# Seven half products for half of gate and value, f32 first loads by SyncE, and fixed orders, in an attention and gated feed-forward kernel

## Chip, core and metric

The kernel runs on one core of one Trainium2 chip. The metric is the device time of one execution in microseconds (us). An execution is profiled apart from the timed ones; its span runs from its first to its last instruction.

## What is computed

Attention over 4 batches, 8 heads, 768 positions and 64 dimensions; three heads (0, 2, 6) are causal over all keys, the other five see only the first 4 keys and a window of 64. Its output, as 3072 tokens of 512, goes through a gated feed-forward layer with a gated residual:

```python
scores = scale * np.matmul(q, k.transpose(0, 1, 3, 2))      # masked, softmax -> a
x = np.matmul(a, v)                                         # -> (3072, 512)
g = x @ w_gate                                              # (512, 1536)
gelu = 0.5 * g * (1.0 + erf(g * inv_sqrt2))
val = x @ w_val                                             # (512, 1536)
ffn_out = gelu * val @ w_out                                # (1536, 512)
res_gate = 1.0 / (1.0 + np.exp(-(x @ w_res)))               # (512, 512)
return x + res_gate * ffn_out
```

## The kernel before

The 3072 tokens are cut into six chunks of 512 (`CHUNKS`, L25; counted from 0 here). For each chunk the kernel computes scores (`scores`, L858), exponentials on ScalarE (L909), masks on VectorE (L945), weighted values on TensorE and normalisation (`weigh`, L998; L1082, L1084), a transposition of x to features (`to_features`, L1104, on TensorE, or by DMA at L1097), gate and value (`gate_value`, L1121), sums of the hidden tile (`sums`, L1175), and output (`output_fast`, L1212; `output`, L1295, for the first two tiles of chunk 0). The text calls TensorE, VectorE, ScalarE, GpSimd and SyncE by the profile's PE, DVE, ACT, POOL and SP as well.

**Gate and value.** Twelve blocks f of 128 features, and for each block four matmuls (one per 128 of the 512 inputs) of 512 tokens for gate and four for value, each in a PSUM bank. ScalarE takes GELU of the gate (L1166), VectorE multiplies it with the value into hT (L1168). In chunk 0 the first four blocks go in two halves of 256 tokens (L1140, L1143).

**Output.** `output_fast` already uses seven half products in place of eight (Strassen's scheme in the form of Winograd) for two tiles of 128 tokens at a time: sums S1 to S4 of hT (L1187), sums T1 to T4 of w_out made once (L1204), products of 256 columns into two PSUM banks, and, between them, copies out of PSUM (`keep`, L1251 and L1252) and additions (`plus`, L1257). Then comes the gate of the residual from tanh (L1226, L1281), the addition of x (L1286) and a store by SyncE (L1292).

**Tiled matmuls.** `mm` (L513) issues a matmul whole (L516) or, when the planner has put the task in column mode, as two of 64 columns of weights each that run beside each other (L517).

**Loads.** Chunks 0 and 1 load queries and keys through GpSimd's DMA queue (L577 is the helper's line for all its DMAs), cast to f16 on the way, and transpose them on TensorE (L709, evicted at L723); later chunks load by GpSimd and transpose by SyncE's DMA (L754). Values and weights come through GpSimd's queue too. While TensorE has nothing else to do at the start, it runs matmuls on a blank tile (L1333).

**Order.** Every instruction or small group is a task with a cost, a priority, buffers and dependencies. `schedule` (L219) replays the kernel in time with the costs of the functions at L458 to L471 and, whenever an engine is free, takes the ready task of the lowest priority; for tasks that several engines can do (`flex`) it picks the one that ends it first. `HINTS` (L46) overrides some priorities. The result is one fixed order for each engine; `assign_waits` and `emit` turn dependencies into semaphore waits. Each engine runs its order without overtaking.

Of the kernel before, what the change touches and what calls it, by code (L numbers as in the profile page):

```python
# [43 lines left out]


HINTS = (  # L46
    "3:-58.9 11:-130.04 428:854.14 430:718.61 444:2782.08 457:-821.9 460:407.45 490:4205.68 521:1522.06 "
    "591:-818.43 610:-36.63 612:486.89 613:-2965.25 619:1544.03 621:-44.07 643:467.87 644:-881 646:4.3 656:119.6 "
    "664:25.04 673:629.62 675:-109.25 695:-2674.26 696:-1856.67 703:-881.5 706:-108.75 707:714.39 708:1939.7 "
    "711:270.02 712:497.18 716:476.22 720:652.56 738:638.32 743:520.23 744:3053.24 749:514.3 750:1799.28 "  # L50
    "751:2383.53 756:521.28 762:1469.72 764:4344.87 767:2237.74 787:-603.93 815:5053.25 817:2978.67 821:1231.87 "
    "824:1484.86 836:2402.62 837:798.1 841:706.04 848:-288.52 849:2997.07 876:2751.74 906:2555.54 913:1516.93 "
    "918:2437.99 919:1519.88 924:1537.25 931:1510.23 936:2384.32 949:2443.79 955:2089.28 967:2846.74 995:-227.38 "
    "1001:29.83 1002:3171.86 1003:3180.29 1004:1146.58 1007:2686.58 1012:1781.89 1040:-803.29 1043:1907.45 "
    "1045:1028.83 1046:667.33 1050:3229.28 1051:1536.45 1053:3573.03 1056:-1823.77 1084:4090.27 1110:2454.97 "
    "1111:2597.62 1117:2808.38 1123:2507.5 1128:2481.58 1129:2529.63 1134:2508.5 1146:2434.73 1152:2779.33 "
    "1153:3034.61 1158:3861.94 1165:2795.06 1171:3076.63 1176:2997.8 1185:5989.69 1188:2243.92 1189:2528.84 "
    "1192:2789.39 1193:2537.45 1194:3836.22 1208:3021.15 1215:6294.68 1263:3219.13 1268:5037.38 1283:4420.5 "
    "1308:4756.92 1311:3513.6 1317:3517.03 1321:3052.3 1329:5930.49 1330:3507.5 1335:3508.5 1336:3519.22 "
    "1341:4624.14 1345:3444.6 1353:3516.64 1354:3538.83 1357:2761.66 1365:3787.63 1366:5173.04 1372:5102.72 "  # L60
    "1386:5438.32 1392:4014.31 1393:4933.66 1418:5146.68 1430:4133.91 1441:5428.8 1452:5127.54 1457:2188.42 "
    "1462:4595.33 1464:5711.23 1467:9389.54 1468:4425.54 ~1471:550.69 1476:5611.77 1499:4504.13 1513:6742.83 "
    "1516:5340.27 1522:4510.5 1523:4585.63 1526:3632.38 1534:4503.02 1539:4253.34 1550:4463.64 1565:7711.51 "
    "1570:4506.5 1571:5085.34 1580:2427.42 1594:2466.44 1610:9272.71 1625:3048.93 1627:6036.71 1629:6167.81 "
    "1631:5064.12 1644:6476.5 1662:4125.72 1671:5044.95 1672:7314.6 1676:4967.2 1683:6427.71 1692:9540.12 "
    "1711:7387.16 1757:5137.62 1784:5507.1 1797:5469.41 1803:7562.23 1817:7773.49 1818:7478.69 1823:7672.83 "
    "1834:7419.08 1836:10250.4 1849:7490.55 "
)

# [121 lines left out]
VS_DMA = 0  # L191
LAT = {"pe": 0.20, "act": 0.10, "dve": 0.08, "pool": 0.12, "sp": 0.1}


class Graph:
# [22 lines left out]

    def schedule(self):  # L219
# [21 lines left out]
        running = []  # L241
        while left:
# [3 lines left out]
            for e in ENGS:  # L246
# [3 lines left out]
                for t in cand[e]:  # L250
# [6 lines left out]
                    key = (int(away), p_, t.seq)  # L257
                    if t.ready > now or (best is not None and key >= bkey):
                        continue
                    if t.alts and any(max(free[f], now) + t.alts[f][0] + BIAS[f] < now + t.alts[e][0] + BIAS[e] - 1e-6  # L260
                                      for f in t.alts if f != e):
                        continue
# [22 lines left out]
                progressed = True  # L285
                if t.name == "g0" and warming:
                    warming = False
                    cand["pe"] = [w for w in cand["pe"] if w.name != "warm"]
                    gone = [w for w in self.tasks if w.name == "warm" and w.end is None]
                    left -= len(gone)  # L290
                    self.tasks = [w for w in self.tasks if w not in gone]
# [109 lines left out]
    def emit(self):  # L401
# [31 lines left out]
        with nc.Block() as blk:  # L433
# [17 lines left out]
            @blk.sync  # L451
            def _(e):
                run("sp", e)
                for t in finals:
                    e.wait_ge(t.sem, 16)
# [6 lines left out]
def c_act(n):  # L462
    return 0.19 + n * 0.000834


def c_dve(n, rate=1.0, psum=True):
    return (0.125 if psum else 0.065) + n * 0.00104 / rate
# [6 lines left out]
def build_kernel(nc, q, k, v, w_gate, w_val, w_out, w_res, out):  # L474
# [11 lines left out]
    scratch = sb("scratch", [128, 1], FP16)  # L486
    blank = sb("blank", [128, 128], FP16)
# [4 lines left out]
    P_vs = Pool(many("vs", 2, [128, NT - 1, NHEAD, DHEAD + 1], FP16))  # L492
    P_vk = Pool(many("vk", 2, [128, 8, DHEAD + 1], FP16))
    P_qkt = Pool(many("qkt", 2, [128, 2, NPAIR, SEQ], FP16))
# [9 lines left out]
    P_hs = Pool(many("hS", 1, [128, 3, NF // 2, 2, 128], FP16))  # L504
    wt = sb("wt", [128, 4, NF // 2, 256], FP16)
    P_ga = Pool(many("gact", 4, [128, 512], FP16))
    P_sr = Pool(many("srs", 3, [128, 512], FP32))
# [5 lines left out]
    def mm(e, o, lhsT, rhs, **k):  # L513
# [8 lines left out]
        "gv": (4, one(6, 7, 5, 4, 3, 2)), "gv0": (4, one(6, 7, 5, 4)), "gvh": (4, one(7, 6, 4, 5)), "out": (2, one(6, 7)), "fin": (4, one(6, 7, 1, 0)), "warm": (1, one(7, 5)),  # L522
# [55 lines left out]

    wtok = {}

    def load_weights():
# [6 lines left out]
        for j in range(4):  # L588
# [3 lines left out]
            wtok["o", j].late = 2.2  # L592
        for nm in "gv":
            for j in range(3):
                wtok[nm, j].late = 2.2 if j else 2.0
# [6 lines left out]
    copies = []  # L602

    def batch(b):
        if b not in batches:
            B_ = B()
            B_.v, B_.vs, B_.vk, B_.qkt = Buf(P_v), Buf(P_vs), Buf(P_vk), Buf(P_qkt)
            B_.vtok, B_.vstok, B_.qtok, B_.ktok = {}, {}, {}, {}

            B_.q6, B_.q6tok = None, {}  # L610
            batches[b] = B_
        return batches[b]

    def values(b, a, z, base, each, on_engines=False):

        BB = batch(b)
        for i in range(a, z):
            BB.vtok[i] = dma("pool", base, 0.9, (lambda i=i: lambda: at(BB.v)[:, i, :, 0:DHEAD])(),
                             v[b, :, i * 128:(i + 1) * 128, :].rearrange("h p d -> p h d"), bufs=[BB.v])
            BB.vtok[i].late = 1.6 if base < 50 else 6.0  # L620
        if a == 0:
# [9 lines left out]
            for t in BB.vktok:  # L631
                t.slack = 12.0 if b else 0.0
# [5 lines left out]
        if on_engines:  # L638
            ts = []
            for lo, hi, pr in ((1, 2, -75),) + (() if VS_DMA else ((2, 4, 130),)):  # L640
                for dst, src, off in ((0, 64, 1), (64, 0, 0)):
                    def vs(on, dst=dst, src=src, off=off, lo=lo, hi=hi):
                        def fn(e):
                            o = at(BB.vs)[dst:dst + 64, lo - 1:hi - 1, :, :].rearrange("p i h d -> p (i h d)")
                            i_ = at(BB.v)[src:src + 64, lo - off:hi - off, :, :].rearrange("p i h d -> p (i h d)")
                            return e.activation(out=o, in_=i_, func=AF.Copy) if on == "act" else e.tensor_copy(out=o, in_=i_)
                        return fn
                    n_ = (hi - lo) * 520
# [9 lines left out]
        for lo in cuts:  # L658
            hi = lo + 1 if each else z
            ts = []  # L660
            for dst, src, off in ((0, 64, 1), (64, 0, 0)):
                ts.append(G.add("sp", 1.2, (lambda lo=lo, hi=hi, dst=dst, src=src, off=off: lambda e: e.dma_start(
                    at(BB.vs)[dst:dst + 64, lo - 1:hi - 1, :, :].rearrange("p i h d -> p (i h d)"),
                    at(BB.v)[src:src + 64, lo - off:hi - off, :, :].rearrange("p i h d -> p (i h d)")))(),
# [7 lines left out]
    def loads_rows(c, si, b, a, z):  # L672
# [17 lines left out]
        for gi, (h0, h1) in enumerate(groups):  # L690
            for j, src in enumerate((q, k)):
                t = dma("pool", base + 4 * gi + j, (h1 - h0) * n * (0.092 if c else 0.089),
# [7 lines left out]
        per = 1 if c == 0 or n == 4 else 2  # L700
        for k_ in range(0, NPAIR, per):
            ps_ = ORDER[k_:k_ + per]
            pr = 1000 * c - 492 + ps_[0] if c else 40 * k_ - 205
            for js in (((1,), (0,)) if c == 0 else ((0, 1),)):
                scr = Buf(P_ps, "scr" if c else "scr0")
                items = [(p, jj) for jj in js for p in ps_]
# [10 lines left out]
                def ev(on, p0=ps_[0], scr=scr, j0=js[0], m=len(items)):  # L717
                    def fn(e):
                        o = at(BB.qkt)[:, :, :, lo:hi].rearrange("c j (y x) w -> c x (j y) w", x=2)[:, p0 % 2]
                        m0 = j0 * 2 + p0 // 2  # L720
                        o = o[:, m0:m0 + m, :].rearrange("c m (p j) -> c m p j", j=n)
# [5 lines left out]
                           bufs=[scr, BB.qkt], name="qkE")  # L727
# [4 lines left out]
    def loads_natural(c, si, b, a, z):  # L732
# [8 lines left out]
        for i in range(a, z):  # L741
            for j, src in ((1, k), (0, q)):
# [9 lines left out]
                for d in ds:  # L752
                    d.late = 5.0
                t = G.add("sp", 1.65, (lambda sv=sv, i=i, j=j: lambda e: e.dma_start(  # L754
                    at(BB.qkt)[:, j, :, i * 128:(i + 1) * 128], sv(), transpose=True))(), ds, base, bufs=[st, BB.qkt], dma=0.85, name="dT")
# [4 lines left out]
            if i == a:  # L760
                values(b, a, z, base, False)
        t = G.add("sp", 0.8, lambda e: e.dma_start(at(BB.q6)[0:64, :, a * 128:z * 128], at(BB.qkt)[64:128, :, 1, a * 128:z * 128]),
                  loaded, base + 1, bufs=[BB.qkt, BB.q6], dma=0.4, name="q6")
        t.late = 1.0
        copies.append(t)
        for i in range(a, z):
            BB.q6tok[0, i] = BB.q6tok[1, i] = t
# [90 lines left out]
    def scores(P, tiles, banks, g, retr):  # L858
# [7 lines left out]
        for bi, (x, blocks, low) in enumerate(banks):  # L866
# [3 lines left out]
            for (b, kt, q0, nq) in blocks:  # L870
# [5 lines left out]
                if kt is None:  # L876
                    deps += [BB.ktok[p, q0]] + ([BB.ktok[p, q0 - 1]] if q0 else [])
                    parts = [(max(0, q0 * 128 - 64 + 64 * s), q0 * 128 + 64 * s, 64, o + 64 * s) for s in range(2)]
                else:
                    deps.append(BB.ktok[p, kt])  # L880
                    parts = [(kt * 128, q0 * 128, nq * 128, o)]
                for i in range(nq):
                    P.where[x, kt, b, q0 + i] = w_ + i * 128
                for (k0, qq, w, oo) in parts:
                    mms.append((lanes[lane], len(mms), BB, half, k0, qq, w, oo, low))
# [5 lines left out]
        def sc(e):  # L891
            side = lambda BB, low, j: at(BB.q6)[:, j, :] if low else at(BB.qkt)[:, j, p, :]
            return [e.matmul(at(scr)[:, oo:oo + w], lhsT=side(BB, low, 1)[half, k0:k0 + 128],  # L893
                             rhs=side(BB, low, 0)[half, qq:qq + w], start=True, stop=True)
                    for (_, _, BB, half, k0, qq, w, oo, low) in mms]
        qkts = [batch(b).qkt for b in dict.fromkeys(b for b, _ in tiles)]
# [548 lines left out]
```

The softmax here doesn't subtract the row's maximum and nothing guards it: scores larger than these inputs give would overflow.

## Time and profile before

| | |
|---|---|
| median of three runs | 265.71 us (265.57 to 266.54) |
| span of the profiled execution | 263.7 us |
| PE, DVE, ACT, POOL busy | 257.7, 181.6, 147.2, 89.3 us |
| bytes read from HBM, written | 29.36 MB, 6.29 MB |
| first matmuls on loaded data | 5.68 us |
| first gate matmuls | 19.72 us |

The profiled execution's time outside its span isn't recorded by itself; the median of the runs lies 2.0 us above the span. Busy time counts overlapping instructions once per engine. A group's line has the code line, engine and operation, the tile written and the tiles read, the shape and the count, then total busy us and mean ns of one, then the engine's idle time just before and who ended it. A matmul's duration includes the time until its last result is out, so matmuls overlap, and the rate is read from the distance of their starts.

### The profile page before, as it was taken

To read this page: it belongs to the slowest core of one execution; us is meant where nothing else is said; L and a number is where in the kernel's file an instruction comes from. 1 tells how busy PE (TensorE), PEld (TensorE's weight loads), DVE (VectorE), ACT (ScalarE), POOL (GpSimd) and SP (SyncE) were. 2 spreads that over 40 slices of the span, in tenths; PEclk is the share of its full clock that TensorE was granted. 3 is DMA by queue.
4 is the path that set the end of the run, shared out by engine and by line. 5 is a ranking of instruction groups with operands and counts; after the bars stand their busy time and mean duration, and the time that the engine had idled before them with its cause. 6 is when DMAs were issued, how large, how long until landed. Compare 5 with 4: busy or idle time off the path is not lost.

```text
span 263.7 us, 7495 instructions
## 1 busy us (share of the span) xinstructions
PE 257.7 (98%) x3226; PEld 164.0 (62%) x3226; DVE 181.6 (69%) x378; ACT 147.2 (56%) x237; POOL 89.3 (34%) x127
## 2 busy tenths in 40 slices
PE   7999999999999999999999999999999999999993
PEld 6777655468444668544567444589655588655692
DVE  2698437798447888557898366888557689837655
ACT  2785467974244987423787242967243888233430
POOL 8999979506109973975000000000000000000003
PEclk9999999999999999999999999999999999999999
DMA  6999999999999999999996110004200004200003
GB/s 83 174 204 206 188 175 231 175 153 204 134 200 148 165 137 177 171 179 176 174 156 150 42 40 0 2 26 101 82 2 0 2 2 122 82 2 0 2 35 127
DMA packets 96513, 29.22 MB, mean 111 GB/s; under 512 B 84449, under 2 KB 93025, under 8 KB 96481
## 3 DMA queue, kind: packets, MB, share of 16 engines
q0 software_dynamic: 70320, 14.69, 67.5%
q1 hardware_dynamic: 26160, 14.07, 28.0%
q8 instruction: 25, 0.41, 0.7%
q14 instruction: 8, 0.06, 0.1%
HBM read 29.36 MB, written 6.29 MB: 135 GB/s over the span
## 4 chain that ended last, share of the span: by engine, by line
PE 95%; DMA 2%; DVE 1%; issue 0%; POOLq 0%
PE ps L516 50%; PE ps L517 32%; PE ps L893 5%; PE ps L1333 2%; PE ps L1017 2%; PE ps L709 2%; DMA qks<-in_q_dram 2%; PE ps L1106 2%; PE ps L984 1%; DVE otile L1281 1%; DVE otile L1286 1%; DVE otile L1257 0%; POOLq L1427 0%
## 5 line engine op out<-in xcount | busy, mean ns | idle before, releaser
L1166 ACT ACTIVATE gact<-ps 128x512 f16<-128x512 f32 x68 | 40.2, 597 | 73.5 <-PE ps L516 43.7
L1168 DVE SCALAR_TENSOR_TENSOR hT<-gact,ps 128x512 f16<-128x512 f16 x68 | 46.1, 686 | 48.0 <-PE ps L516 23.1
L516 PE MATMUL ps<-xT,wg 128*128 128x512 f16 (+1 forms) x208 | 50.0, 363 | 0.0
L516 PE MATMUL ps<-xT,wv 128*128 128x512 f16 (+1 forms) x202 | 49.0, 362 | 0.0
L1286 POOL TENSOR_TENSOR otile<-otile,xtok 128x256 f32<-128x256 f32 x3 | 2.4, 801 | 136.2 <-DVE otile L1281 136.2
L577 POOL DMA_DIRECT2D qks<-in_k_dram x36 | 28.0, 810 | 17.3 <-DMA qkt<-qks 13.9
L516 PEld LDWEIGHTS ps<-xT,wg 128*128 128x128 f16 x208 | 20.1, 98 | 20.0 <-DVE otile L1257 0.3
L516 PEld LDWEIGHTS ps<-xT,wv 128*128 128x128 f16 x202 | 19.4, 98 | 20.0 <-DVE hT L1168 0.5
L577 POOL DMA_DIRECT2D qks<-in_q_dram x36 | 28.4, 828 | 2.2 <-issue 1.4
L517 PE MATMUL ps<-xT,wv 128*64 128x512 f16 x204 | 28.3, 380 | 0.0
L577 POOL DMA_DIRECT2D va<-in_v_dram x24 | 21.3, 920 | 15.1 <-PE ps L516 15.1
L517 PE MATMUL ps<-xT,wg 128*64 128x512 f16 x192 | 26.3, 379 | 0.0
L909 ACT ACTIVATE ea<-ps 128x1024 f16<-128x1024 f32 (+2 forms) x24 | 21.1, 915 | 1.7 <-PE ps L893 1.6
L1257 DVE TENSOR_TENSOR otile<-otile,ps 128x256 f32<-128x256 f32 x33 | 13.6, 417 | 7.1 <-PE ps L517 4.7
L1226 ACT ACTIVATE srs<-ps 128x512 f32<-128x512 f32 x22 | 13.1, 595 | 9.1 <-PE ps L517 6.7
L517 PEld LDWEIGHTS ps<-xT,wv 128*64 128x64 f16 x204 | 11.5, 110 | 9.8 <-DVE hT L1168 0.3
L1084 DVE TENSOR_TENSOR xtok<-ps,rcp 128x512 f32<-128x512 f32 (+1 forms) x28 | 16.8, 606 | 0.2
L517 PEld LDWEIGHTS ps<-xT,wg 128*64 128x64 f16 x192 | 11.1, 110 | 9.0
L893 PE MATMUL ps<-qkt 64*128 64x64 f16 (+4 forms) x391 | 16.4, 213 | 0.0
L893 PEld LDWEIGHTS ps<-qkt 64*128 64x128 f16 x391 | 9.8, 94 | 8.0 <-issue 4.2
L516 PE MATMUL ps<-wo,hT 128*128 128x256 f16 (+1 forms) x84 | 14.4, 304 | 0.0
L1286 DVE TENSOR_TENSOR otile<-otile,xtok 128x512 f32<-128x512 f32 (+1 forms) x21 | 14.3, 691 | 0.2
(109 smaller groups left out, 437.4 us busy)
## 6 DMA issues: line engine op xcount, KB each, us to landing
out_dram<-otile SPq DMA_DIRECT2D x22, 256.0 KB, 2.4
va<-in_v_dram POOLq DMA_DIRECT2D x24, 128.0 KB, 17.6
qks<-in_k_dram POOLq DMA_DIRECT2D x32, 64.0 KB, 12.6
qks<-in_q_dram POOLq DMA_DIRECT2D x32, 64.0 KB, 13.0
wg<-in_moe_w_gate_dram POOLq DMA_DIRECT2D x3, 512.0 KB, 10.2
wv<-in_moe_w_val_dram POOLq DMA_DIRECT2D x3, 512.0 KB, 12.1
wo<-in_moe_w_out_dram POOLq DMA_DIRECT2D x4, 384.0 KB, 22.8
vs<-va SPq DMA_DIRECT2D x4, 260.0 KB, 7.9
```

The costliest lines, as they stand in the source:

```text
L516: return e.matmul(o, lhsT=lhsT, rhs=rhs, **k)
L517: return [e.matmul(o[h:h + 64], lhsT=lhsT[:, h:h + 64], rhs=rhs, **k) for h in (0, 64)][-1]
L577: return G.add(eng, issue, lambda e: e.dma_start(out_ap(), in_ap), deps, prio, bufs=bufs, dma=cost, name=name, grp=grp)
L709: return [e.transpose(out=at16(scr)[64 * x:64 * x + 64, (m * n + i) * 128:(m * n + i + 1) * 128], in_=piece(jj, h, i), identity=ident[:, : ...
L893: return [e.matmul(at(scr)[:, oo:oo + w], lhsT=side(BB, low, 1)[half, k0:k0 + 128], rhs=side(BB, low, 0)[half, qq:qq + w], start=True, sto ...
L909: return e.activation(out=o, in_=i_, func=AF.Exp, scale=SM_SCALE)
L1084: t2 = G.add("dve", c_dve(2 * n * 64), lambda e: e.tensor_tensor(out=xview(), in0=avv(0, DHEAD), in1=scale(), op=ALU.mult), [t1] + xdeps, ...
L1166: ta = G.add("act", c_act(512), (lambda gb=gb, ga=ga: lambda e: e.activation(out=at(ga)[:, :], in_=at(gb)[:, :], func=AF.Gelu))(), [tg], p ...
L1168: th = G.add("dve", c_dve(512), (lambda vb=vb, ga=ga, f=f: lambda e: e.scalar_tensor_tensor(out=hv(f), in0=at(ga)[:, :], scalar=0.5, in1=a ...
L1226: tas.append(G.add("act", c_act(512), (lambda rb=rb, sr=sr: lambda e: e.activation(out=at(sr)[:, :], in_=at(rb)[:, :], func=AF.Tanh, scale ...
L1257: return G.add("dve", c_dve(256), lambda e: e.tensor_tensor(out=dst(), in0=dst(), in1=at(D)[:, 0:256], op=ALU.add), [t, k], pr, bufs=[D, o ...
L1286: fn = (lambda ot=ot, lt=lt, w=w: lambda e: e.tensor_tensor(out=at(ot)[:, w], in0=at(ot)[:, w], in1=at(xbuf)[:, lt, w], op=ALU.add))()
```

## The change

**Products.** In chunks 1 to 5, blocks 0 to 5 stay plain, and blocks 6 to 11 are done in three pairs (6 with 9, 7 with 10, 8 with 11) with seven products of 256 inputs, 128 features and 256 tokens in place of eight, for gate and for value: six groups a chunk. The sums of weights (`gv_sums`) are made once in chunk 0, the sums of x (`fast`, name `xS`) in every chunk. A group works in one of three "lanes" of two PSUM banks. Blocks 0 to 2 use the lanes first; blocks 3 to 5 are ordered after the output products of the chunk before. Scores of the next chunk are ordered after the last of these groups.

```diff
+NP = 3
+FA, FB = NF - 2 * NP, NF - NP
+LANES = 3
...
+        "lane": (LANES, [(4, 5), (2, 3), (0, 1)]),
...
+            t15 = product([("A11", "B11", AL, True), ("S1", "T1", AR, False)], list(free))
+            seed = copy((lambda ps=ps: at(ps)[:, BL]), (lambda ps=ps: at(ps)[:, AL]), [t15], [ps], "seed")
+            hold = copy((lambda es=es: at(es)[:, 0:256]), (lambda ps=ps: at(ps)[:, AR]), [seed], [ps, es], "hold")
+            t6 = product([("S2", "T2", BL, False)], [seed])
+            m1 = merge(AR, [t6, hold])
+            t7 = product([("S3", "T3", BL, False)], [m1])
+            t23 = product([("A12", "B21", AL, False), ("S4", "B22", AR, False)], [m1])
+            m2 = merge(BR, [t7])
+            t4 = product([("A22", "T4", BL, False)], [m2])
```

A product is two matmuls of 256 columns. `copy` is a flex task of ScalarE or VectorE on 256 columns, `merge` a VectorE addition of 256 columns from and to PSUM with the held tile, which is one of the four output tiles (`P_ot`). GELU and the multiplication with the value then read both banks of the lane, 512 columns at a time, and release it.

**First loads.** In chunk 0, queries and keys of heads 0 to 3 come as f32 by four DMAs of SyncE into one of the x tiles, and ScalarE or VectorE casts them:

```diff
+            f32 = Buf(P_x)
+            for m in range(2):
+                for j, src in ((1, k), (0, q)):
...
+                    t = G.add("sp", 0.52, (lambda w_=w_, src=src, m=m: lambda e: e.dma_start(
+                        w_(), src[b, m:m + 3:2, lo:hi, :].rearrange("h (p j) d -> p h (j d)", j=n)))(), [], -200 + o_,
+                        bufs=[f32], dma=0.01, name="ld32")
...
+                    tc = G.flex({"dve": (c_dve(512, 1.0, False), cast("dve")), "act": (c_act(512), cast("act"))}, [t],
```

Heads 4 to 7 stay on GpSimd's queue, which now begins with them. The transpositions of chunk 1 are evicted in larger pieces (four pairs of heads at a time).

**GpSimd.** For chunks 3 to 5 masks, casts of x, sums of x and sums of hT may run on VectorE or on GpSimd:

```diff
+            tm = G.flex({e_: (d_, fn) for e_, d_ in (("dve", c_dve(w * L, 1.8 if L == 2 else 1.5, False)), ("pool", 0.25 + 0.0021 * w * L))[:2 if P.c > 2 else 1]},
```

**Stores.** In chunks 1 to 5, but for the last two tiles, x is stored by one DMA of SyncE per chunk as soon as it is there, and the gated product is added to it in DRAM by an accumulating DMA of GpSimd, which waits for that store. The addition of x on VectorE and SyncE's store of the tile are gone there:

```diff
+            if c >= ACCUM and not end:
+                t = G.add("pool", 1.0, (lambda ot=ot, r0=r0: lambda e: e.dma_start(out[r0:r0 + 128, :], at(ot)[:, :], accum_op=ALU.add))(),
+                          ends + [stored[c]], pr - 3000, bufs=[ot], dma=1.0, name="out")
```

**Order.** `HINTS` is emptied. `PLAN` holds one list of task numbers for each engine, in the order PE, ACT, DVE, POOL, SP, and `schedule` follows it; the lists also fix which engine does a flex task. The planner's costs for ScalarE and VectorE are rewritten.

```diff
+                offers = cand[e]
+                if queue:
+                    offers = [t for t in queue[e][heads[e]:heads[e] + 1] if t in offers] + [t for t in offers if t.name == "warm"][:1]
```

**Smaller edits.** Queries and keys have buffers of their own (two `kT` per batch, two `qT` of one chunk) in place of one joint `qkt`, and the copy to `q6` is two DMAs. The shifted copy of v leaves out head 0. The third sum of w_out is written in place, so that `wt` has three parts. There are two tiles for tanh instead of three, and the sums of hT are split into `hS` (first four pairs) and `wS` (last two), where `wS` also takes the sums of x. Warm-up matmuls have 256 columns instead of 128. A task that depends on one DMA of a group now depends on all of it.

## The prediction

> **What bounds the kernel now.** I read the page first (busy shares, slices, chain), then the matmul timeline for prices, the groups kept apart by shape, the windows by stage, and last the start and the tail.
>
> ```profile
> PE 257.7 (98%) x3226; PEld 164.0 (62%) x3226; DVE 181.6 (69%) x378; ACT 147.2 (56%) x237; POOL 89.3 (34%) x127
> ...
> PE   7999999999999999999999999999999999999993
> ...
> DMA  6999999999999999999996110004200004200003
> ...
> PE 95%; DMA 2%; DVE 1%; issue 0%; POOLq 0%
> ```
>
> TensorE is busy in every slice and is 95% of the chain that ended last. In the chain from 25 us to 257.35 us the only pieces that are not TensorE's are two of 0.02 to 0.03 us. So a microsecond of matmul taken out there is a microsecond of time, as long as nothing else becomes late. DMA is full until slice 21 (about 145 us), but TensorE doesn't wait for it after the start.
>
> Two stretches of the matmul timeline give the prices (start us, us, then the group):
>
> ```profile
> 198.85 0.60 PE L517 MATMUL ps<-xT,wv 128*64 128x512 f16 x4
> 199.28 0.60 PE L517 MATMUL ps<-xT,wg 128*64 128x512 f16 x4
> ...
> 252.91 0.82 PE L517 MATMUL ps<-wo,hT 128*64 128x256 f16 x12
> 253.45 0.99 PEld L517 LDWEIGHTS ps<-wt,hS 128*64 128x64 f16 x18
> 253.56 1.15 PE L517 MATMUL ps<-wt,hS 128*64 128x256 f16 x18
> ```
>
> The next group starts 0.43 us after four half-array matmuls, which are two full ones of 512 columns: 0.216 us each. Twelve halves of 256 columns, six full ones, take 0.65 us: 0.109 us each. Narrow matmuls cost no more per column. The durations of 273 and 380 ns in the groups hold some 165 ns of draining and are used only for latency.
>
> ```profile
> L1257 DVE TENSOR_TENSOR otile<-otile,ps 128x256 f32<-128x256 f32 x33 | 13.6, 417 | 7.1 <-PE ps L517 4.7 <-PE ps L516 2.0
> L1286 DVE TENSOR_TENSOR otile<-otile,xtok 128x512 f32<-128x512 f32 x20 | 13.4, 684 | 0.2
> L1252 ACT ACTIVATE otile<-ps 128x256 f32<-128x256 f32 x18 | 6.7, 380 | 5.5 <-PE ps L517 3.9 <-PE ps L516 1.5
> L1251 DVE COPY otile<-ps 128x256 f32<-128x256 f32 x15 | 6.3, 423 | 2.4 <-PE ps L517 1.3 <-PE ps L516 1.0
> ```
>
> These are the prices of a merge (417 ns), a copy out of PSUM (380 on ScalarE, 423 on VectorE) and of the residual add that goes (684).
>
> Two windows of chunk 1, attention and then gate and value:
>
> ```profile
> 45.00:64.00 19.00, 19.00 (x250) 12.06 (x243) 16.16 (x34) 15.27 (x26) 6.98 (x10) 1.00 2.02 172
> 64.00:85.00 21.00, 21.00 (x109) 9.74 (x107) 12.76 (x22) 7.10 (x13) 8.44 (x12) 1.00 1.60 170
> ```
>
> Columns: window, length, then PE, PEld, DVE, ACT, POOL busy. VectorE carries 85% in attention without holding TensorE up, and has 8.2 us free beside gate and value.
>
> The start:
>
> ```profile
> 1.32 0.91 POOL L577 DMA_DIRECT2D qks<-in_q_dram  x1 [0.80 <-POOLq L1427]
> ...
> 5.68 0.64 PE L709 MATMUL ps<-ident,qks 128*64 128x128 f16 x16 [0.69 <-DMA qks<-in_q_dram]
> ...
> 10.06 0.77 POOL L577 DMA_DIRECT2D wg<-in_moe_w_gate_dram  x1
> ```
>
> The first real work waits until 5.68 us for a load from GpSimd's queue. From there to 19.7 us, where gate and value begin, the pieces of L1333 (warm-up matmuls that fill holes) add up to about 6.2 us of the chain: the start is bound by data, not by TensorE.
>
> **What the Trainium skill says.** "TensorE: Matmul & The Clock Gate", Back-to-back issue gap: a lone matmul of N columns takes N/2.4 + 2.5 ns, 109 ns for 256 and 216 for 512. The trace agrees (0.109, 0.216 us); the page's shorter 131 ns for streams of 512 is not seen here. "SBUF — State Buffer", SBUF: two separate sides: VectorE with two SBUF inputs and GpSimd lock each other out of a shared port. The tail agrees:
>
> ```profile
> 258.21 0.84 POOL L1286 TENSOR_TENSOR otile<-otile,xtok 128x256 f32<-128x256 f32 x1 [0.78 <-DVE otile L1281]
> 258.50 0.83 DVE L1286 TENSOR_TENSOR otile<-otile,xtok 128x256 f32<-128x256 f32 x1
> ```
>
> VectorE needs 0.83 us for 256 columns there, where 512 columns take 0.684 undisturbed. "DMA: Bandwidth & Descriptors", SWDGE vs HWDGE vs iDMA: casting or adding during a DMA is for GpSimd's queue alone. So SyncE's f32 loads need casts on an engine, and the accumulating stores must go to GpSimd; the trace of before has every casting load on POOL and no accumulate.
>
> **Part by part.**
>
> Seven products. In chunks 1 to 5 six of twelve column blocks change, in three pairs, for gate and for value: 30 groups. Before, one such pair took 2 blocks x 4 matmuls of 512 columns: 8 x 0.216 = 1.73 us. Now it takes 7 products x 2 matmuls of 256: 14 x 0.109 = 1.53 us. Saved: 0.20 us x 30 = 6.1 us, all on the path.
>
> Their price is hand-overs. Each group adds two copies (seed, hold) and two merges. VectorE: 60 merges x 0.417 = 25.0 us, 20 sums of x (128x512 f16, 0.42 as in L1187) = 8.4, eight sums of weights once, 768 elements each, between 0.42 (512) and 0.69 (1024), say 0.55 = 4.4; the 60 copies are shared, 0.38 each on ScalarE or 0.42 on VectorE. In one chunk's gate-and-value stretch (now 96 x 0.216 - 1.2 = 19.5 us of TensorE): 12.8 + 5.0 + 1.7 = 19.5, less about two residual adds (1.4) = 18.1 us if all copies go to ScalarE (7.1 + 4.6 = 11.7), 20.6 if half stay. So VectorE goes from 61% to 93% or more in this stretch.
>
> One group's chain on its lane: first two products end 0.60 after their start (three starts of 0.109 and one duration 0.273), seed 0.38, two merges 0.417 each, three further pairs of matmuls 0.38 each, two last reads (GELU 2 x 0.60 or product with value 2 x 0.69), with 0.05 to ScalarE or VectorE and 0.15 back to TensorE (0.05 between L709 and L723 at 10.81 us; 0.12 to 0.15 between L1082 or L945 and TensorE at 16.7 and 15.6 us): about 5.0 us. Three lanes hold 3 x 1.53 = 4.6 us of matmuls, so a round alone would stall 0.4 us; three plain blocks (5.2 us of matmuls a chunk) are there to fill this. A stall of 0 to 0.5 us in each of ten rounds, 0 to 5 us: I take 2.0, since VectorE at 85% cost nothing in attention but 93% with a chain in series is new. The trace shows no such chain, so both ends stay in the range.
>
> Loads at the start. Four f32 loads of 256 KB on SyncE's otherwise empty queue, beside two 0.8 us issues fewer on GpSimd. The nearest row is the 256 KB store from SyncE, 2.4 us to landing. Issued at about 0.8 us, the first lands near 3.2 us; a cast (0.39 on VectorE, L1091; about 0.6 on ScalarE) makes first work possible at about 3.8 us against 5.68: 1.9 us. Heads 4 to 7 are issued 2.1 us earlier on POOL, values and weights 1.7 us earlier. Bytes are no fewer, so DMA could take some of it back; and holes of 6.2 us could shrink by more than the shift. Between 0 and 5 us; I take 2.5.
>
> Stores. 18 residual adds of 0.684 (12.3 us of VectorE, hidden behind TensorE) give way to five stores of x on SyncE and 18 accumulating stores on POOL. No row prices these; from nothing to 1 us of POOL each plus a landing of some 3 us. Queued behind them on POOL are loads of later chunks: chunk 5's last is issued at 121 us for scores at 204, so they can wait. Their output tile comes free later; there are four, now also used for the held copies. If that cover is gone, the wait is part of the 0 to 5 us above. On the path: 0.
>
> Masks, casts and sums on POOL in chunks 3 to 5, where POOL is idle from about 124 us: 801 ns for 256 columns (L1286) against about half on VectorE. They relieve VectorE but slow its SBUF-to-SBUF work by the lock: 0. The separate buffers for q and k, larger evictions in chunk 1, smaller copies of v, wider warm-ups: 0 on the path. Two tanh buffers instead of three and one shared sum buffer: inside the stall term. The order lists cost nothing themselves; they set how well the chains interleave. The tail (last matmul work at 259.5 us, then VectorE and a store) keeps its code: 0.
>
> Sum on the profiled span: 263.7 - 6.1 - 2.5 + 2.0 = 257.1 us. The median 265.71 lies 2.0 us above this span, and I carry this over: 259.1, told as 259.0.
>
> **Rivals.** (1) VectorE becomes the bound beside gate and value: 20.6 us of work in 19.5, plus waits in order, about 1 us a chunk, with the round stalls of 0.4: 5 us in all, 262. For: 93% or more of VectorE; the lock. Against: copies can go to ScalarE, sums to POOL. (2) Slower: a lane's round trip decides. If neither plain blocks nor scores fill, and the merges queue behind other VectorE work (one 0.69 us piece ahead of each of seed, first and second merge adds 2.1 us), each of ten rounds stalls 0.4 + 2.1 - 1.0 filled = 1.5 us: 15 us against 8.6 saved, 272. It makes the kernel slower from 0.86 us a round. Against: orders are fixed in advance and can keep merges first. (3) The start gives nothing, as DMA is as full as before and four casts sit in front: 263.7 - 6.1 + 2.0 + 2.0 = 261.6.
>
> **Chances.** Forecast 0.64; VectorE bound 0.14; start without gain 0.11; slower 0.11. An outcome within 0.5% (about what a measurement can tell from no change), 264.4 to 267.0, takes 0.03 from the edges of the second and third; faster 0.86, slower 0.11. The range 254.5 to 264 reaches from no stalls and a start gain of 5 us (254.6) to rival 1 with little start gain; the slower case is left out.
>
> **What would show it.** First transposition near 4 us and gate and value near 17 us; 420 matmuls of 256 columns on the new products (twice as many halves in tiled stretches); TensorE idle of about 2 us between 25 us and the end, on merges and seeds; VectorE busy between 190 and 210 us (181.6 + 25.0 + 8.4 + 4.4 - 12.3, plus its share of copies, less what POOL takes). I'm wrong if that idle passes 6 us, or if the start keeps its 19.7 us.

## The result and the profile after

The changed kernel takes 286.25 us (median of 4 runs, 284.04 to 288.11) against 265.64 us (265.57 to 266.54) for the kernel before: ratio 1.076, interval 1.0717 to 1.0804. The forecast was 259.0 us. The profiled execution took 286.25 us with a span of 284.5 us, 20.8 us more than before. Line numbers are those of the changed kernel unless said otherwise.

The page of the changed kernel: busy times, four rows of its slices, and the chain of work that ended last.

```profile
PE 259.1 (91%) x3414; PEld 182.0 (64%) x3414; DVE 207.9 (73%) x433; ACT 166.2 (58%) x295; POOL 135.0 (47%) x164
...
PE   6799999999999999929987999869999999999990
...
PEclk9599999999999999998997999999999999999997
DMA  6999999997999999999249999704880004470025
...
PE 78%; DVE 10%; DMA 7%; ACT 1%; POOL 1%; issue 1%; SPq 0%; POOLq 0%; DVEq 0%
```

TensorE, busy in every slice before, now has holes, and DVE and DMA hold 17% of the chain where they held 3%. The span minus TensorE's busy time was 263.7 - 257.7 = 6.0 us and is 284.5 - 259.1 = 25.4 us: 19.4 of the 20.8 us are idle time. The other 1.4 us are busy time, in which two things are set against each other. The trace has TensorE at half clock for 6.8 us from 7.9 us on, and for 3.4 us from 127.4 and from 151.3 us on; before, it ran at full clock until the last matmul. Work done in 13.6 us at half clock would take 6.8 us at full clock. So the busy time should rise by up to 6.8 us for the clock and fall by 6.1 for the seven products, 0.7 us in all; the other 0.7 us (warm-up matmuls changed too) are not accounted for.

What TensorE waited for in the changed kernel (total us, times, longest):

```profile
PE ps L590 <- DVE ps L1364: 5.1, 1, 5.1
PE ps L591 <- DVE hS L1412: 3.5, 3, 1.8
PE ps L820 <- ACT qks L793: 2.8, 1, 2.8
PE ps L590 <- DVE eb L1061: 2.1, 1, 2.1
PE ps L1577 <- DVE blank L624: 1.1, 1, 1.1
PE ps L590 <- DVE hT L1412: 1.1, 1, 1.1
```

The wait for blank is the program's first and stood there before. The other five are new, and fall into three places.

**The start.** The four f32 loads from SyncE, in the view of the tile they land in:

```profile
L784 SPq DMA_DIRECT2D xtok<-in_q_dram x2: 452/452/453, 0.8 to 1.3; - x2
L784 SPq DMA_DIRECT2D xtok<-in_k_dram x2: 462/472/481, 1.8 to 2.3; - x2
L793 DVE CAST qks<-xtok x2: 433/490/548, 3.7 to 9.5; 128x512 f16<-128x512 f32 x2
...
DMA to landing us min/median/max: 2.8/4.6/7.1
```

and TensorE beside them (start, length, idle time before it in brackets):

```profile
5.03 0.64 PE L820 MATMUL ps<-ident,qks 128*64 128x128 f16 x16
5.60 0.28 PE L1577 MATMUL ps<-blank 128*128 128x256 f16 x1
8.64 0.64 PE L820 MATMUL ps<-ident,qks 128*64 128x128 f16 x8 [2.76 <-ACT qks L793]
```

The queries landed 2.9 and 3.0 us after their issue (the forecast took 2.4 us), and the first transposition is earlier (5.03 against 5.68 us). The keys, issued 1 us later, took 6.1 and 7.1 us, to 7.94 and 9.47 us of the span. Nothing goes on without them, and gate and value begin at 25.0 us instead of 19.7.

**Chunk 2.** The last output tiles of chunk 1 are stored at 112 to 115 us, and chunk 2's gate and value want tiles for held copies soon after. GpSimd's queue, ScalarE, VectorE and TensorE, picked from the timeline:

```profile
112.35 0.92 POOL L1522 DMA_DIRECT2D out_dram<-otile  x1 [3.08 <-DVE wS L1327]
...
113.82 1.26 POOL L1522 DMA_DIRECT2D out_dram<-otile  x1
...
126.24 0.38 ACT L1360 ACTIVATE otile<-ps 128x256 f32<-128x256 f32 x1 [6.15 <-DMA out_dram<-otile]
...
126.72 0.43 DVE L1364 TENSOR_TENSOR ps<-ps,otile 128x256 f32<-128x256 f32 x1 [5.46 <-ACT otile L1360]
...
127.21 0.50 PE L590 MATMUL ps<-xs,wg 128*128 128x256 f16 x2 [5.06 <-DVE ps L1364]
```

The store issued at 113.82 us landed 12.4 us later. Until then its tile could not take the held copy; the copy held up the merge, and the merge held up TensorE. Half clock followed at once. The median landing of the 18 accumulating stores is 5.7 us.

**Chunks 3 to 5.** GpSimd's mask and VectorE's mask of the same chunk meet:

```profile
147.50 3.30 DVE L1061 TENSOR_TENSOR ea<-ea,m_causal 128x1024 f16<-128x1024 f16 x1
147.78 2.46 POOL L1061 TENSOR_TENSOR es<-es,m_win 128x1024 f16<-128x1024 f16 x1
...
151.19 0.49 PE L590 MATMUL ps<-va,eb 128*128 128x65 f16 x6 [2.12 <-DVE eb L1061]
```

The VectorE instruction takes 0.69 us when alone; here it lasts until just after GpSimd's ends. At 182.40 us a sum on VectorE (L1412, 128x1024) takes 3.22 us while two sums and a mask of GpSimd's run, and at 142.43 us one of 0.42 us takes 1.68.

The end is longer too. TensorE's last matmul ends 7.8 us before the span does, against 4.2 us before. The last accumulating store is issued at 278.00 us, 1.2 us after the last matmul, and lands 4.7 us later; before, SyncE's last store was issued 1.7 us after the last matmul and landed 2.0 us later. Then GpSimd's queue drains, from its last issue to 284.30 us:

```profile
L503 POOLq DRAIN  x1: 6325/6325/6325, 278.0 to 278.0; - x1
```

The drain ends 1.6 us after the last landing, here and in every run below whose last stores GpSimd issues. In the kernel before it ended 0.5 us ahead of the last landing.

In the one stretch with none of this, from the last transposition of x in chunk 1 to that in chunk 2, the changed kernel is faster: 39.4 us (69.28 to 108.64) against 41.4 us (63.66 to 105.05).

### The profile page after: what moved, and what is told of

Read it like the earlier page. It is cut to its first block, busy times and chain, and to the rows that moved or that the text cites. A ratio compares the mean times of both kernels' runs of the same rounds, so it can differ in the third digit from the quotient of the medians.

```text
span 284.5 us, 8074 instructions
## 1 busy us (share of the span) xinstructions
PE 259.1 (91%) x3414; PEld 182.0 (64%) x3414; DVE 207.9 (73%) x433; ACT 166.2 (58%) x295; POOL 135.0 (47%) x164
## 4 chain that ended last, share of the span: by engine, by line
PE 78%; DVE 10%; DMA 7%; ACT 1%; POOL 1%; issue 1%; SPq 0%; POOLq 0%; DVEq 0%
PE ps L590 41%; PE ps L591 25%; DMA out_dram<-otile 4%; PE ps L1009 4%; DVE hS L1412 3%; DMA xtok<-in_k_dram 3%; PE ps L1135 2%; PE ps L1577 2%; PE ps L820 2%; PE ps L1224 2%; DVE ea L1061 1%; DVE hT L1412 1%; DVE otile L1518 1%; PE ps L1102 1%; POOL out_dram L1522 1%
## 5 line engine op out<-in xcount | busy, mean ns | idle before, releaser
L590 PE MATMUL ps<-xT,wg 128*128 128x512 f16 (+1 forms) x172 | 38.1, 342 | 0.1
L590 PE MATMUL ps<-xT,wv 128*128 128x512 f16 (+1 forms) x168 | 37.6, 338 | 0.0
L1364 DVE TENSOR_TENSOR ps<-ps,otile 128x256 f32<-128x256 f32 x60 | 24.9, 429 | 17.3 <-ACT otile L1360 7.6
L1292 DVE SCALAR_TENSOR_TENSOR hT<-gact,ps 128x512 f16<-128x512 f16 x38 | 25.8, 685 | 12.3 <-PE ps L590 4.1
L1522 POOL DMA_DIRECT2D out_dram<-otile x18 | 16.9, 1089 | 26.6 <-DVE otile L1518 14.4
L652 POOL DMA_DIRECT2D va<-in_v_dram x24 | 25.0, 1060 | 8.1 <-PE ps L590 7.9
L590 PEld LDWEIGHTS ps<-xT,wg 128*128 128x128 f16 x172 | 16.5, 99 | 12.4 <-DVE hT L1292 1.1
L1025 ACT ACTIVATE ea<-ps 128x1024 f16<-128x1024 f32 (+2 forms) x24 | 21.5, 919 | 4.4 <-PE ps L1009 4.4
L590 PE MATMUL ps<-wo,hT 128*128 128x256 f16 (+1 forms) x114 | 19.9, 299 | 1.1 <-DVE hT L1412 1.1
L591 PE MATMUL ps<-xT,wv 128*64 128x512 f16 (+1 forms) x152 | 19.3, 346 | 0.0
L591 PE MATMUL ps<-xT,wg 128*64 128x512 f16 (+1 forms) x144 | 17.5, 344 | 0.0
L1494 DVE TENSOR_TENSOR otile<-otile,ps 128x256 f32<-128x256 f32 x33 | 13.5, 418 | 5.1 <-PE ps L591 3.1
L1009 PE MATMUL ps<-qT,kT 64*128 64x64 f16 (+4 forms) x391 | 17.1, 216 | 0.0
L1412 POOL TENSOR_TENSOR hS<-hT 128x1024 f16<-128x1024 f16 x2 | 4.2, 2120 | 26.6 <-DVE hT L1292 14.0
```

The source lines that it names most:

```text
L590: return e.matmul(o, lhsT=lhsT, rhs=rhs, **k)
L591: return [e.matmul(o[h:h + 64], lhsT=lhsT[:, h:h + 64], rhs=rhs, **k) for h in (0, 64)][-1]
L652: return G.add(eng, issue, lambda e: e.dma_start(out_ap(), in_ap), deps, prio, bufs=bufs, dma=cost, name=name, grp=grp)
L1009: return [e.matmul(at(scr)[:, oo:oo + w], lhsT=side(BB, qb, low, 1)[half, k0:k0 + 128], rhs=side(BB, qb, low, 0)[half, qq:qq + w], start=T ...
L1025: return e.activation(out=o, in_=i_, func=AF.Exp, scale=SM_SCALE)
L1292: th = G.add("dve", c_dve(512), (lambda vb=vb, ga=ga, f=f, vw=vw: lambda e: e.scalar_tensor_tensor(out=hv(f), in0=at(ga)[:, :], scalar=0.5 ...
```

## The experiments

My theory was that three parts of the change, each a side matter of the forecast, cost time independently: the accumulating stores, the work moved to GpSimd, and the f32 loads. The rival was that the seven products with their hand-overs lose by themselves. All ratios are to the kernel before in runs on the same chip; the changed kernel's is 1.076.

**One part undone at a time.** First the stores, in two steps.

```
-  e.dma_start(out[r0:r0 + 128, :], at(ot)[:, :], accum_op=ALU.add)      # on GpSimd
+  e.dma_start(out[r0:r0 + 128, :], at(ot)[:, :])                        # e1_plain: on GpSimd; e1_sp: on SyncE
```

> The 18 accumulating stores stay on GpSimd's queue, in the same places, but write plainly (the residual x is left out of the sum, so the output lacks it). Theory A (the addition in DRAM is what takes 12.4 us to land and holds the output tile that the held copy of chunk 2 needs): the 5.1 us idle of TensorE at 121 us goes, with the half-clock stretch after it; about 279 us. Theory B (the queue is what is slow: the store stands behind value loads and beside the 1 MB store of x while the DMA engines are full): landing stays at 10 us or more and the time within 1% of 286 us.

> The same 18 tiles are stored plainly by SyncE instead (x left out of the sum), in the same places of the fixed order. Theory B (GpSimd's queue): landing falls to 2 to 4 us, the 5.1 us idle goes and about 6.5 us with its slow clock: 279 to 280 us. Theory A, if it alone is right, gives the same here and in the run before. Rival C (chains and fixed orders stall TensorE whatever the store does): the wait moves elsewhere, over 283 us.

Measured: e1_plain 1.0564 (1.0522 to 1.0606), with a median landing of 4.0 us and 1.3 us of waiting for a merge; e1_sp 1.0226 (1.0165 to 1.0286), with a landing of 3.1 us and no wait for a merge. SyncE's plain stores take away 0.053 of the 0.076, and GpSimd's plain stores 0.020 of it. The tail falls from 7.8 us to 5.4 and 3.4. Issues of output tiles on the pages of the changed kernel, of e1_plain and of e1_sp, with the median us to landing (the last line has four of SyncE's earlier stores in it; the 18 alone have 3.1 too):

```profile
out_dram<-otile POOLq DMA_DIRECT2D x18, 256.0 KB, 5.7
...
out_dram<-otile POOLq DMA_DIRECT2D x18, 256.0 KB, 4.0
...
out_dram<-otile SPq DMA_DIRECT2D x22, 256.0 KB, 3.1
```

The median hides the store that mattered. The one that took 12.4 us in chunk 2 took 9.9 us in e1_plain and 4.3 us in e1_sp. So at that place the larger part comes with its issue by GpSimd and the smaller part with the addition. Theory A of e1_plain expected 279 us and theory B a landing of 10 us or more with no gain; the 282 us lie between them.

Then the work on GpSimd. e2_dve changes the order lists only: 20 masks, casts and sums (the expectations count 18) stand in VectorE's list instead of GpSimd's, at the same planned times.

```
-  GpSimd:  1159 1169 1247 1321 1322 1324 1386 1385 1486 1553 1556 1559 1560 1629 1621 1654 1721 1724 1791 1797
+  VectorE: 1159 1169 1247 1321 1322 1324 1386 1385 1486 1553 1556 1559 1560 1629 1621 1654 1721 1724 1791 1797
```

And the start (e3_start):

```
-  f32 = Buf(P_x)
...
-  for gi, (h0, h1) in list(enumerate(groups))[c == 0:]:
+  for gi, (h0, h1) in enumerate(groups):
```

> The 18 masks, casts and sums that GpSimd took go back to VectorE, each where GpSimd was to start it; nothing else is moved. Theory L (the lock between VectorE and GpSimd stretches VectorE's two-input work from 0.69 to 3.2 us and TensorE waits for it): idle of TensorE in chunks 3 to 5 falls from about 8 us to under 3, and with the clock about 7 us are won: 279 us. Rival V (VectorE is short of time, which is why they were moved): the 18 pieces (about 10 us on VectorE) push its chain and nothing is won, 286 us or more.

> Queries and keys of heads 0 to 3 of chunk 0 come through GpSimd's queue with its cast again, ahead of the rest; casts on engines are gone. Theory S (the f32 loads share the DMA engines with GpSimd's loads and land up to 9.5 us, and TensorE waits with its clock halved): first scores near 8 us, gate and value near 20 us instead of 25, about 281 us. Rival (the start is bound by values and weights whichever way queries come): within 0.5% of 286 us.

Measured: e2_dve 1.0588 (1.0539 to 1.0637), e3_start 1.0643 (1.0572 to 1.0713), with gate and value at 21.5 us. The gains, some 4.6 and 3.1 us, are smaller than the 7 and 5 expected, but the rivals expected none. The waits of TensorE that are left in e2_dve:

```profile
PE ps L593 <- DVE ps L1367: 6.3, 2, 5.4
PE ps L823 <- ACT qks L796: 2.5, 1, 2.5
PE ps L1580 <- DVE blank L627: 1.1, 1, 1.1
```

(L1367 is the merge, L796 the cast.) TensorE's waits for sums and masks, 6.7 us in all, are gone but for one of 0.2 us, and VectorE's busy time fell from 207.9 to 203.8 us although it executes 20 instructions more. GpSimd cost VectorE more time than it took off it.

**All three undone.** This is the test of the rival. The edits of e1_sp, e2_dve and e3_start are made together; the seven products stay.

> The changed kernel with all three suspects undone at once: its 18 accumulating stores become plain stores by SyncE (x is left out of these 18 tiles of the output), its 18 masks, casts and sums of chunks 3 to 5 go back to VectorE, and queries and keys of chunk 0 are loaded by GpSimd's casting loads again. The seven products and their lanes stay. Theory (three separate causes that add up): the ratio to the kernel before is 1.076 less 0.053 less 0.017 less 0.012, about 0.994, TensorE is idle for less than 9 us, no idle gap of over 1.8 us is left, and so no stretch at half clock before the tail. Rival (the seven products with their hand-overs are themselves a loss): the ratio stays above 1.01, with waits for seeds and merges in every chunk.

Measured: 0.9916 (0.9894 to 0.9937). Page and waits of e7_three:

```profile
PE 254.9 (97%) x3431; PEld 181.0 (69%) x3431; DVE 202.9 (77%) x451; ACT 164.6 (63%) x293; POOL 90.4 (34%) x128
...
PEclk9999999999999999999999999999999999999999
```

```profile
PE ps L1559 <- DVE blank L627: 1.1, 1, 1.1
PE ps L1117 <- DMA vs<-va: 1.0, 1, 1.0
PE ps L594 <- DVE otile L1470: 0.4, 1, 0.4
```

TensorE has full clock and 7.3 us of idle time, and it waits for no merge or seed in any chunk. The five stores of x by SyncE are still in this kernel, so by themselves they are not the loss. The three gains, 0.053, 0.017 and 0.012, sum to 0.082; undone together they gave 0.084. The rival falls, with one reservation: e7_three leaves out the 18 residual adds. The last two kernels below have them.

**One part put back.** From the other side, one of the three edits is taken back on top of the other two:

> The kernel with all three suspects undone, and one put back: the 18 masks, casts and sums of chunks 3 to 5 on GpSimd (the 18 output tiles are stored without x, as there). Theory (the port lock alone costs what undoing it gained, 0.017): ratio to the kernel before about 1.009, between 1.003 and 1.018, with TensorE waits on hS, hT and a mask of 6 us in all. Rival (the lock only hurt because the other two had made everything late): ratio as without it, 0.992, and no such waits.

> The kernel with all three suspects undone, and one put back: the 18 accumulating stores by GpSimd, with x stored first by SyncE. Theory (a held copy that waits for an output tile whose store has not landed, then half clock, then a longer tail): ratio 1.035 to 1.055, one wait of 3 to 6 us on a merge in chunk 2, half clock after it, and a tail of some 7 us from TensorE's last matmul to the end. Rival (the stores hurt only beside the other two): ratio below 1.01.

> The kernel with all three suspects undone, and one put back: queries and keys of heads 0 to 3 of chunk 0 by SyncE as f32 with casts on the engines (the 18 output tiles are stored without x, as there). Theory (keys land at 8 to 9.5 us, a gap of over 2 us and 6.8 us of half clock in the start): ratio about 1.004, between 0.998 and 1.010. Rival (warm-up matmuls and data-bound work fill the start anyway): ratio as without it, 0.992.

Measured: x1_pool 1.0185 (1.0148 to 1.0222), x3_f32 1.0024 (1.0009 to 1.0039). The four runs of x2_acc lie between 274.49 and 283.02 us, too far apart for an interval; the shortest is 1.033 of the kernel before, their median, 280.41 us, 1.055. So each part hurts alone: 0.027 for GpSimd's work (more than the 0.017 expected, though TensorE's waits for sums came to 3.6 us and not 6, and none was for a mask), 0.011 for the loads, and for the stores 0.041 by the shortest run, 0.063 by the median. In the profiled run of x2_acc, which took 279.69 us, the first wait is the merge again, and its tail is 8.3 us:

```profile
PE ps L593 <- DVE ps L1346: 6.3, 2, 4.6
PE ps L1117 <- DMA vs<-va: 1.8, 1, 1.8
PE ps L593 <- DMA xT<-x: 1.2, 1, 1.2
```

**Why the keys landed late.** Only GpSimd's order list changes: its nine small constants first, its loads after them.

```
-  5 219 3 2 218 220 6 221 248 4 222 7 8 223 9 199 10 202
+  5 3 2 6 4 7 8 9 10 219 218 220 221 248 222 223 199 202
```

> The changed kernel with one edit: GpSimd makes its nine small constants first and issues its first casting load after them, some 3 us later. SyncE's four f32 loads are as they were. Theory (the f32 loads were slow because GpSimd's loads share the DMA engines with them): keys land by about 4.5 us instead of 7.9 and 9.5, TensorE's gap of 2.8 us at 5.9 us and the half clock after it go; GpSimd's later loads cost up to 3 us in place of it, so the ratio lies between 1.065 and 1.080. Rival (the f32 loads of keys are slow by themselves): keys land no earlier than 7.5 us, and the time rises by up to 3 us, ratio 1.076 to 1.088.

Measured: 1.0723 (1.0699 to 1.0747). The f32 tile in e8_masks:

```profile
L787 SPq DMA_DIRECT2D xtok<-in_k_dram x2: 462/466/470, 1.8 to 2.3; - x2
L796 DVE CAST qks<-xtok x2: 426/537/648, 3.6 to 6.9; 128x512 f16<-128x512 f32 x2
...
DMA to landing us min/median/max: 2.8/3.7/4.5
```

The same loads, issued at the same time, land after at most 4.5 us where they took up to 7.1. (I had expected them at 4.5 us of the span, and overlooked that they are issued at 1.8 and 2.3.) TensorE's gap of 2.76 us and the half clock after it are gone. So the loads were slow because of GpSimd's loads beside them. The Trainium skill, "DMA: Bandwidth & Descriptors", Issuing engines are not separate DMA queues, says that all issuing engines feed the same 16 DMA engines; the two landings agree. The time hardly falls. Gate and value begin at 22.9 us, 2.1 us earlier, but the span is only 0.8 us shorter; that GpSimd's loads, now later, took the rest back is likely and not shown.

**How the stores do their harm.** The held copies get three tiles of their own, in the room of the third sum of output weights, which is written over the second (so some output products use a wrong sum, with the same instructions):

```
+  P_hd = Pool(many("hold", 3, [128, 256], FP32))
-  es = Buf(P_ot)
+  es = Buf(P_hd)
```

> The changed kernel with one edit: the held copies of the lanes get three tiles of their own instead of output tiles. The room comes from the output weights' sums, of which the third is written over the second, so two products of the output stage read the same sums. All accumulating stores stay. Theory (the accumulating store does its harm by keeping the output tile that the next held copy needs): the wait of 5.1 us on a merge in chunk 2 goes, and the half clock after it; ratio about 1.050. Rival (the accumulating stores do their harm by themselves, in GpSimd's queue and on the DMA engines): TensorE's waits stay as they were, ratio 1.070 or more.

Measured: 1.0584 (1.0547 to 1.0622), between the two theories and nearer the first (1.050) than the second (1.070). The wait for a merge is gone, although the store took 12.5 us here:

```profile
PE ps L821 <- ACT qks L794: 2.8, 1, 2.8
PE ps L591 <- DVE eb L1062: 2.1, 1, 2.1
PE ps L592 <- DVE hS L1413: 2.0, 2, 1.8
```

The shared tile is worth 0.018, a third of what the stores cost. Of the rest the longer tail is 7.8 - 3.4 = 4.4 us, some 0.016 by this estimate. What is left, about 0.02, I take to be GpSimd's queue: 18 issues of 1.09 us stand between its masks and sums, and the wait for the mask of eb, 2.1 us here, is gone in e1_sp and in x1_pool, where GpSimd makes masks and stores nothing. No run tested this alone, so it stays argued.

**The products alone, with x.** Two kernels compute the whole reference with the edits of e2_dve and e3_start, and with residual adds on VectorE and plain stores by SyncE in every chunk, as before. Both follow an order made for them, and they differ from each other in that order only.

```
-ACCUM = 1
+ACCUM = 99
```

> The seven products and their lanes alone, with the whole of the reference computed: all three suspects undone, the residual adds back on VectorE and plain stores by SyncE, and an order of the instructions searched for this. Theory (the products give about 4 us from chunk 1 on, and 16 adds of 0.684 us find room beside TensorE, VectorE at some 81%): ratio 0.985 to 1.000. Rival (11 us more of VectorE make it the bound): ratio 1.015 to 1.035.

> As f_correct, which was 1.0026 of the kernel before, with another order of the same instructions: in f_correct the copies of v by SyncE in chunk 1 landed 6.7 to 7.5 us after their issue, and TensorE waited 1.4 us for them, and gate and value began at 21.2 us against 19.7 before. The order was searched again with a later landing for these copies and for an earlier end of chunk 1. Theory (f_correct lost its 2.5 us of gain from chunk 1 on to some 3.3 us in the start and chunk 1, and most of these come back): ratio 0.990 to 0.998. Rival (VectorE's 11 us of residual adds have used up the gain): ratio 1.000 to 1.004.

(The adds are 18, not 16, so 12.3 us, not 11.) Measured: f_correct 1.0026 (1.0016 to 1.0036), f_two 0.9995 (0.9985 to 1.0006). Neither meets its theory's range; f_two lies at the lower edge of its rival's. Busy times of f_two and its first wait:

```profile
PE 256.4 (97%) x3422; PEld 180.7 (68%) x3422; DVE 212.7 (80%) x468; ACT 166.3 (63%) x294; POOL 90.5 (34%) x128
```

```profile
PE ps L801 <- DMA qks<-in_k_dram: 1.3, 1, 1.3
```

TensorE is idle for 8.5 us (7.3 in e7_three), its busy time is 1.5 us higher, and the gain of 0.008 is gone. VectorE is busy 9.8 us more than in e7_three, but after the first 18 us TensorE's longest wait for it is 0.2 us. With x, then, the products neither lose nor win over the whole kernel. Where the time goes is seen in three stretches. From the last transposition of x in chunk 1 to the last matmul f_two takes 260.15 - 67.50 = 192.7 us and the kernel before 259.51 - 63.66 = 195.8 us, so the products gain 3.2 us there with the adds in place. But f_two reaches that transposition 3.8 us later, and its tail is 0.6 us longer. Half of the 3.8 us is there when gate and value begin: at 21.6 us in e7_three and f_two and 21.2 in f_correct, against 19.7 before. What delays them by 1.5 to 1.9 us in kernels that load as before did stays open (in e7_three the first transposition is 1.3 us later, in f_two it is not). No version here beats the kernel before by more than e7_three's 0.008, and that one leaves out x.

## Why the prediction was wrong

The forecast was 6.6 us less, and the kernel took 20.6 us more. What the sum took for the products and their hand-overs holds; what it took for the loads, the stores and GpSimd's work does not.

**Seven products, 6.1 us on the path: priced right.** A pair of the new matmuls starts every 0.22 us in the trace (118.87, then 119.09).

**Hand-overs, 0 to 5 us, taken 2.0: right in size.** From the last transposition of x in chunk 1 to the last matmul, e7_three takes 258.79 - 66.92 = 191.9 us and the kernel before 195.8: 4.0 us gained, where 6.1 - 2.0 = 4.1 was forecast. That is without the residual adds; with them f_two gains 3.2 us. Over its whole span e7_three gains only 1.5 us (262.2 against 263.7; the medians say 2.2, 0.008), since it reaches that transposition 3.3 us late, 1.8 of them at the first gate and value, and ends with a tail 0.8 us shorter. VectorE is busy 19.66 of 23 us around chunk 1's gate and value in the changed kernel (67 to 90 us), 85%, not 93%, and TensorE lost nothing there. "VectorE at 85% cost nothing in attention but 93% with a chain in series is new" was the wrong thing to fear.

**Loads at the start, 0 to 5 us gained, taken 2.5: wrong in sign.** The step built on "SyncE's otherwise empty queue". The queue was empty, but GpSimd's loads were under way beside it: the keys took up to 7.1 us, and at most 4.5 us when those loads came later. The sentence "Bytes are no fewer, so DMA could take some of it back" named the cause but put its lower end at nothing. Measured: first gate and value 5.3 us later, of which 3.6 us go when the loads alone are undone (21.5 us in e3_start), and 0.011 to 0.012 (some 3 us) lost at the end.

**Stores, "On the path: 0": wrong, and the largest error.** The step had the mechanism in hand: "Their output tile comes free later; there are four, now also used for the held copies." It priced "a landing of some 3 us", with 2.4 us for stores of SyncE in the kernel before at hand. Accumulating stores from GpSimd took 5.7 us in the median and 12.4 at worst, that one beside a store of x of 1 MB and loads. And it put the loss inside the 0 to 5 us of the stalls, beside which 0.053 (14 us) is another size. Each accumulate was bounded at 1 us of GpSimd and cost 1.09, but 18 of them in a queue that now also held masks were not followed to who waits behind them.

**Masks, casts and sums on GpSimd, "0": wrong.** The text cited the lock of the shared port (the Trainium skill, "SBUF — State Buffer", SBUF: two separate sides), saw 0.83 us for 256 columns in the tail where 512 take 0.684, set this against the relief of VectorE, and wrote 0. But the locked instructions were sums and masks that TensorE needs next. The price was not VectorE's time but the latency of one instruction: 3.30 us for 0.69. This part costs 0.017 to 0.027.

**Tail, "keeps its code: 0": wrong by 3.6 us.** The code of the last pair is the same, but the pair before it now ends in accumulating stores of GpSimd. The last of them lands 2.7 us longer after its issue than SyncE's last store did, and GpSimd's drain puts the end 1.3 us further behind the last landing; the issue itself comes 0.4 us sooner after the last matmul.

**The clock: not in the sum at all.** The kernel before had no hole, so no slice of its page showed a lower clock.

The rival that ended slower, 272 us by the lane's round trip, had the right sign for a wrong reason: it was round trips and merges queued on VectorE, and the merge that came late waited for a store. The signs by which the prediction said that it would be wrong did show it: TensorE's idle time between 25 us and its last matmul is 13.5 us, where over 6 us was named, and gate and value begin even later than the 19.7 us before.

## What to carry to other kernels

When work moves from an engine that is full to one that is idle, price its landing, not its occupation: a store on a slower path holds its tile until it lands, a load on an empty queue shares the DMA engines with the full one, and GpSimd's elementwise work can stretch the one VectorE instruction that TensorE waits for. An order fixed in advance cannot step around such errors: it was made for other landings and latencies, and each engine waits in its place. Where a kernel keeps TensorE at 98%, add to every possible hole of 2 us or more the half clock that comes with it.

## What the runs showed of the hardware

**A hole of 1.8 us can halve the clock.** The Trainium skill, "TensorE: Matmul & The Clock Gate", Part 1, puts the step to half rate after an idle window of some 3.4 us; the holes here that did it were often shorter. In the traces of the changed kernel and of the experiments, every one of fifteen holes of 2.1 us or more brought half clock for 3.41 or 6.83 us, which began inside the hole or up to 2.5 us after it. Of nine holes of 1.77 to 1.84 us five did (e1_sp at 175.0 us, for one) and four did not (the changed kernel at 183.8 us); no hole of 1.62 us or less did by itself. By these lengths a hole of 2 us costs up to 1.7 or 3.4 us on top; this is an estimate, half of 3.41 and of 6.83 us.

**Landing times by path.** The same 256 KB tile landed after 5.7 us (accumulating, GpSimd), 4.0 us (plain, GpSimd) and 3.1 us (plain, SyncE), all medians of 18 stores in otherwise equal kernels. The spread is wide: the longest were 12.4, 9.9 and 4.4 us.

**The instruction recorded as first can be the one that waits.** VectorE's mask started at 147.50 us by the trace, 0.28 us ahead of GpSimd's, and still ended 0.56 us after it, having taken 3.30 us for 0.69.

**GpSimd's own last stores delay the end.** In the seven runs whose last stores GpSimd issues, its final drain ended 1.6 us after the last of them landed.
